# Attention masks of the second batch: from identity products on TensorE to additions on VectorE

## The chip, the cores and the metric

One core of a Trainium2 chip runs the whole program. The metric is the device time of one execution in microseconds (us); lower is better. PE is TensorE's matmul stream and PEld its weight loads, DVE is VectorE, ACT ScalarE, POOL GpSimd and SP the engine that issues most transfers.

## What is computed

Two batches of causal attention with 8 heads, 576 positions and 64 values per head, then two feed-forward layers over the 1152 tokens. Heads 0 to 3 see the last 32 positions ("local"), heads 4 to 7 the positions that agree with theirs modulo 32 ("strided").

```python
scores = scale * np.matmul(q, k.transpose(0, 1, 3, 2))
mask_local = (rel >= 0) & (rel < stride)
mask_strided = (rel >= 0) & (pos[None, :] % stride == pos[:, None] % stride)
scores = np.where(masks[None, :, :, :], scores, -1000000000.0)
scores = scores - np.max(scores, axis=-1, keepdims=True)
attn = np.exp(scores)
attn = attn / (np.sum(attn, axis=-1, keepdims=True) + 1e-09)
return np.matmul(attn, v).astype(np.float32)
# then x = attention output as [tokens, 512]:
#   four experts: sum over e of p[:, e] * (relu(x @ w1[e]) @ w2[e])
#   a gated layer: (sigmoid(x @ w_gate) * (x @ w_val)) @ w_out
```

## The kernel before

**Groups and stages.** Attention is cut into 32 groups, 16 for each batch. A strided group holds four blocks of 72 x 72 scores (288 values on each of 72 partitions), a local group three blocks of 96 x 128 (384 values on each of 96 partitions). The groups pass through the stages of `STAGES`, one group a step: scores (for two groups at every second step, `pair_scores`), maximum and exponentials (`group_exp`), normalisation one step later (`group_norm`), transposition three steps later (`group_transpose`), products with the values at five (`group_values`), and the split into a high and a low half, `xh` and `xl` (`group_split`). The generator `attention` gives this order, and `attend` takes one step of it.

**Scores.** `pair_scores` takes a bank of PSUM for each of the two groups. In each it first multiplies the identity by the mask (line 723, `start=True`), which writes 0 or -1e9 into every score, and then adds the products of queries and keys block by block (line 736, `start=False`). Three banks named `sps` serve all groups. `group_exp` lets VectorE take the negated row maximum from the bank (`nm`); ScalarE then exponentiates block by block, with `nm` as bias and the row sum into `sm`. `group_norm` adds 1e-9 to the sums and inverts them on VectorE (two short instructions on `sm`), and GpSimd multiplies (`P` by `sm`).

**What runs between.** The first batch's attention runs almost alone. The second batch's steps are mixed into the first four matrix stages (`early_up` and `early_down`, first expert, first 384 tokens): after each step of a stage (three products, lines 893 to 895) a share of 0.36 of an attention step is due. These stages need weights in two halves: ScalarE copies the raw weight (`wh`), GpSimd subtracts (`wl`, used by line 895). One piece of that work follows every second step of a stage. The results of `early_up` are evacuated by ScalarE (`hh`) and then VectorE (`hl`), those of `early_down` by VectorE into `x2acc`. Four PSUM banks (`gp`) serve these stages, the transposes of queries and keys (`qkps`), of probabilities (`tps`), and a few others.

**Order.** The order on each engine is that in which the program issues, and each engine keeps its order. `Ledger` books an estimated cost for every instruction of VectorE, ScalarE and GpSimd. After the attention, the order of background work follows from this account; the account's clock is then set to the latest of the three engines (line 1349) and all later decisions are made against that clock. During the attention, the order is that of `attend` and of `early_step`. Instructions of these three engines pass through a helper, so their rows all carry its line, 102, and are told apart by their tiles.

Of the kernel before, what the change touches and what calls it, by code (L numbers as in the profile page):

```python
# [17 lines left out]
ALU = mybir.AluOpType  # L18
# [89 lines left out]
def attn_moe_glu_kernel(ctx, tc, q, k, v, dp, w1, w2, wg, wv, wo, out):  # L108
    nc = tc.nc
    ledger = Ledger()  # L110
    dve, act, pool_ = (Reckoned(e_, name, ledger) for e_, name in ((nc.vector, "V"), (nc.scalar, "A"), (nc.gpsimd, "G")))
# [136 lines left out]
    identb = const.tile([128, 128], BF16, tag="identb", name="identb")  # L248
# [447 lines left out]
    def qk_local(b, part):  # L696
        for nm, dst in (("ql", QT), ("kl", KT)):
# [13 lines left out]
            else:  # L711
                dve.tensor_copy(dd, ps[:, :384])

    def pair_scores(pair):


        tiles = []
        for kind, b, c, half, hh in pair:
            ps = sp_.tile([128, 512], F32, tag="s", name="sps")
            n, w, m = (NU, NU, 4) if kind == "s" else (96, 128, 3)  # L720
            pv_ = ps[:n, :m * w].rearrange("p (a b) -> p a b", b=w)
            mask = mask_s.unsqueeze(1).to_broadcast([NU, 4, NU]) if kind == "s" else mask_l[:, half:half + 3, :]
            nc.tensor.matmul(pv_, identb[:n, :n], mask, start=True, stop=False)  # L723
            soft[kind, b, c, half, hh] = (pv_, n, w, m)
            tiles.append(pv_)
        m = soft[pair[0]][3]
        for j in range(m):
            for pv_, (kind, b, c, half, hh) in zip(tiles, pair):
                if kind == "s":
                    lo = 64 * half  # L730
                    qs_, ks_ = QT["s", b, c, hh][lo:lo + 64, j, :], KT["s", b, c, hh][lo:lo + 64, j, :]
                else:
                    lo, i = 64 * c, 3 * half + j
                    q0, k0 = hh * S + 96 * i, hh * S + max(96 * i - 32, 0)
                    qs_, ks_ = QT["l", b][lo:lo + 64, q0:q0 + 96], KT["l", b][lo:lo + 64, k0:k0 + 128]
                nc.tensor.matmul(pv_[:, j, :], qs_, ks_, start=False, stop=j == m - 1)  # L736

    def group_exp(g):
        pv_, n, w, m = soft[g]
        nm = atp.tile([128, 4], F32, tag="nm", name="nm", bufs=4)  # L740
        sm = atp.tile([128, 4], F32, tag="sm", name="sm", bufs=4)
        pt = atp.tile([128, 384], F32, tag="P", name="P", bufs=3)
        pp = pt[:n, :m * w].rearrange("p (a b) -> p a b", b=w)
        dve.tensor_reduce(nm[:n, :m], pv_, AX.X, ALU.max, negate=True)
        for j in range(m):
            act.activation(
                pp[:, j, :], pv_[:, j, :], AF.Exp, bias=nm[:n, j:j + 1], accum_out=sm[:n, j:j + 1]
            )
        soft[g] = (pp, sm[:n, :m], n, w, m)
# [72 lines left out]
    def attention():  # L822

        gs = []
        for b in range(B):
            gs += [("s", b, c, half, hh) for c in range(2) for hh in range(2) for half in range(2)]
            gs += [("l", b, c, half, hh) for half in range(2) for hh in range(2) for c in range(2)]
        n = len(gs)
        stage = dict(values=group_values, transpose=group_transpose, scores=pair_scores,
                     exp=group_exp, norm=group_norm, split=group_split)  # L830

        def ends():
# [583 lines left out]
```

## Time and profile before

| | |
|---|---|
| median of 3 runs | 649.19 us (648.48 to 649.87) |
| the profiled execution's own time | 648.63 us |
| its span, first to last instruction | 646.9 us |
| busy: PE / DVE / ACT / POOL | 636.3 / 438.7 / 341.9 / 266.7 us |
| granted TensorE clock | 0.999 of full speed |

The profile records one execution; its own time is 1.7 us longer than its span. Times in it are counted from the first instruction. A busy time is a union of intervals; what an engine waited for is inferred from semaphores. Second-batch scores are computed between 45.8 and 87 us; before that lie the first batch's attention and the loads, behind it the matrix stages to the end.

### The profile page before, as it was taken

To read this page: it belongs to the slowest core of one execution; us is meant where nothing else is said; L and a number is where in the kernel's file an instruction comes from. 1 tells how busy PE (TensorE), PEld (TensorE's weight loads), DVE (VectorE), ACT (ScalarE), POOL (GpSimd) and SP (SyncE) were. 2 spreads that over 40 slices of the span, in tenths; PEclk is the share of its full clock that TensorE was granted. 3 is DMA by queue.
4 is the path that set the end of the run, shared out by engine and by line. 5 is a ranking of instruction groups with operands and counts; after the bars stand their busy time and mean duration, and the time that the engine had idled before them with its cause. 6 is when DMAs were issued, how large, how long until landed. Compare 5 with 4: busy or idle time off the path is not lost.

```text
span 646.9 us, 12698 instructions
## 1 busy us (share of the span) xinstructions
PE 636.3 (98%) x4897; PEld 468.1 (72%) x4897; DVE 438.7 (68%) x882; ACT 341.9 (53%) x808; POOL 266.7 (41%) x311
## 2 busy tenths in 40 slices
PE   8889999999999999999999999999999999999998
PEld 5678889999676666666666666667978877987794
DVE  4876677787461886693887779898866759633432
ACT  6757643554753646775655454653565574542230
POOL 4675661000422325361435345440465367453540
PEclk9999999999999999999999999999999999999999
DMA  9976131040431544261674564254113832330002
GB/s 185 231 167 158 41 121 35 1 130 2 143 109 34 175 132 159 97 191 34 197 261 131 171 213 147 99 163 146 35 34 122 292 141 76 106 131 1 33 19 98
DMA packets 48884, 77.00 MB, mean 119 GB/s; under 512 B 19540, under 2 KB 24440, under 8 KB 47672
## 3 DMA queue, kind: packets, MB, share of 16 engines
q1 hardware_dynamic: 48824, 76.20, 38.7%
q8 instruction: 38, 0.62, 0.4%
q14 instruction: 22, 0.18, 0.1%
HBM read 59.66 MB, written 16.53 MB: 118 GB/s over the span
## 4 chain that ended last, share of the span: by engine, by line
PE 95%; DVE 3%; ACT 1%; issue 1%; POOL 0%; POOLq 0%; ACTq 0%
PE gps L893 23%; PE gps L895 23%; PE gps L894 23%; PE gps L997 19%; PE sps L736 1%; PE o L786 1%; PE tps L762 1%; ACT P L102 1%; PE warm L265 1%; DVE nm L102 1%; DVE sm L102 1%; PE qkps L682 0%; PE sps L723 0%; PE qkps L704 0%; DVE xh L102 0%
## 5 line engine op out<-in xcount | busy, mean ns | idle before, releaser
L102 POOL TENSOR_TENSOR hl<-t,hh 128x384 f16<-128x384 f32 x72 | 76.6, 1067 | 178.1 <-ACT t L102 174.2
L997 PEld LDWEIGHTS <-w 128*128 128x128 f16 x1512 | 125.0, 98 | 1.8
L997 PE MATMUL gps<-x,w 128*128 128x192 f16 x1512 | 126.2, 246 | 0.0
L893 PE MATMUL gps<-x,w 128*128 128x384 f16 x288 | 93.9, 326 | 0.0
L894 PE MATMUL gps<-x,w 128*128 128x384 f16 x288 | 93.9, 326 | 0.0
L895 PE MATMUL gps<-x,w 128*128 128x384 f16 x288 | 93.9, 326 | 0.0
L893 PE MATMUL gps<-hh,w 128*128 128x384 f16 x288 | 93.9, 326 | 0.0
L894 PE MATMUL gps<-hl,w 128*128 128x384 f16 x288 | 93.9, 326 | 0.0
L895 PE MATMUL gps<-hh,w 128*128 128x384 f16 x288 | 93.9, 326 | 0.0
L893 PEld LDWEIGHTS <-w 128*128 128x128 f16 x576 | 56.4, 98 | 37.3 <-issue 0.2
L895 PEld LDWEIGHTS <-w 128*128 128x128 f16 x576 | 56.4, 98 | 37.2
L894 PEld LDWEIGHTS <-w 128*128 128x128 f16 x576 | 56.4, 98 | 36.4
L102 ACT ACTIVATE hh<-gps 128x384 f16<-128x384 f32 (+1 forms) x96 | 46.7, 486 | 49.2 <-PE gps L895 48.8
L102 POOL TENSOR_TENSOR stage<-magn,stage 128x512 f16<-128x512 f32 x36 | 45.4, 1268 | 45.3 <-ACT magn L102 38.9
L102 ACT ACTIVATE w<-raw,up 128x512 f16<-128x512 f32 x48 | 32.0, 715 | 34.9 <-DVE up L102 34.8
L102 ACT ACTIVATE P<-sps,nm 72x72 f32<-72x72 f32 (+1 forms) x112 | 36.3, 331 | 23.7 <-DVE sm L102 15.6
L102 ACT ACTIVATE bits<-raw 128x512 f32<-128x512 f32 x36 | 24.3, 674 | 38.1 <-DVE magn L102 37.8
L102 DVE SCALAR_TENSOR_TENSOR w<-raw,up,w 128x512 f16<-128x512 f32 x48 | 40.1, 871 | 5.1 <-ACT w L102 4.9
L102 POOL TENSOR_TENSOR sg<-four,sg 128x384 f32<-128x384 f32 x9 | 9.8, 1093 | 80.6 <-DVE four L102 80.6
L893 PE MATMUL gps<-w,hh 128*128 128x512 f16 (+1 forms) x112 | 41.6, 371 | 0.0
L895 PE MATMUL gps<-w,hl 128*128 128x512 f16 (+1 forms) x112 | 41.6, 371 | 0.0
L894 PE MATMUL gps<-w,hh 128*128 128x512 f16 (+1 forms) x112 | 41.6, 371 | 0.0
(146 smaller groups left out, 1278.9 us busy)
## 6 DMA issues: line engine op xcount, KB each, us to landing
raw<-in_moe_w_dram SPq DMA_DIRECT2D x32, 512.0 KB
raw<-in_moe_w_gate_dram SPq DMA_DIRECT2D x12, 512.0 KB
raw<-in_moe_w_val_dram SPq DMA_DIRECT2D x12, 512.0 KB
raw<-in_moe_w_out_dram SPq DMA_DIRECT2D x12, 512.0 KB
wg<-stage SPq DMA_DIRECT2D x21, 256.0 KB
wv<-stage SPq DMA_DIRECT2D x21, 256.0 KB
w<-wg SPq DMA_DIRECT2D x3, 1024.0 KB
wo<-stage SPq DMA_DIRECT2D x12, 256.0 KB
```

The costliest lines, as they stand in the source:

```text
L102: return f(*a, **k)
L265: nc.tensor.matmul(ps, zero.to_broadcast([128, 128]), zero.to_broadcast([128, 512]), start=True, stop=True,)
L736: nc.tensor.matmul(pv_[:, j, :], qs_, ks_, start=False, stop=j == m - 1)
L762: nc.tensor.transpose(pv_[:, j, :], pp[:, j, :], ident[:n, :n])
L786: nc.tensor.matmul(o[x * 64:x * 64 + 64, j * n:(j + 1) * n], lhsT, tts[x][:, j, :], start=True, stop=True)
L893: nc.tensor.matmul(ps, ah, bh, start=first and i == 0, stop=False)
L894: nc.tensor.matmul(ps, ah, bl, start=False, stop=False)
L895: nc.tensor.matmul(ps, al, bh, start=False, stop=last and i == n - 1)
L997: nc.tensor.matmul(o, l_, r_, start=first and x + kk + y == 0, stop=last and x * kk * y == 2, skip_group_check=True)
```

## The change

In groups of the second batch (`b > 0`) the product of identity and mask is no longer issued. Every score block is then written by a product of its own with `start=True`. Ahead of the maximum, `group_exp` adds the mask to the scores on VectorE, which reads the bank and writes the same bank. The mask stays in its SBUF tile of type bfloat16 (for the strided groups repeated by its access pattern). The first batch keeps the products.

```diff
+    masks = {}
+
     def pair_scores(pair):
...
-            nc.tensor.matmul(pv_, identb[:n, :n], mask, start=True, stop=False)
+            if b == 0:
+                nc.tensor.matmul(pv_, identb[:n, :n], mask, start=True, stop=False)
+            else:
+                masks[kind, b, c, half, hh] = mask
             soft[kind, b, c, half, hh] = (pv_, n, w, m)
...
-                nc.tensor.matmul(pv_[:, j, :], qs_, ks_, start=False, stop=j == m - 1)
+                nc.tensor.matmul(pv_[:, j, :], qs_, ks_, start=b > 0, stop=b > 0 or j == m - 1)
...
     def group_exp(g):
...
+        if g in masks:
+            dve.tensor_tensor(pv_, pv_, masks.pop(g), ALU.add)
         dve.tensor_reduce(nm[:n, :m], pv_, AX.X, ALU.max, negate=True)
```

## Rows read from the trace of the kernel before

**Rows 1.** The page: the chain that ended last, by engine.
```profile
PE 95%; DVE 3%; ACT 1%; issue 1%; POOL 0%; POOLq 0%; ACTq 0%
```
**Rows 2.** Stretches: window, length, busy us of PE, PEld, DVE, ACT, POOL; clock, DMA.
```profile
44.00:55.00 11.00, 10.04 (x96) 8.89 (x95) 5.96 (x15) 7.30 (x32) 4.97 (x5) 1.00 0.83 189
55.00:65.00 10.00, 10.00 (x104) 8.97 (x102) 7.01 (x20) 6.91 (x36) 5.89 (x7) 1.00 0.34 104
75.00:91.00 16.00, 16.00 (x149) 13.51 (x148) 10.44 (x30) 9.54 (x40) 11.58 (x14) 1.00 0.17 47
```
**Rows 3.** Chain in order of time, mask products: start us, us on the chain, what.
```profile
45.99 0.25 PE sps L723 x2
...
68.05 0.33 PE sps L723 x2
```
**Rows 4.** DVE in order of time: start us, us, instruction, [idle before <-releaser].
```profile
39.24 0.46 DVE L102 TENSOR_TENSOR xl<-o,xh 128x288 fp32r<-128x288 f32 x1
...
50.56 0.16 DVE L102 TENSOR_SCALAR sm<-sm 72x4 f32<-72x4 f32 x1
50.75 0.17 DVE L102 RECIPROCAL sm<-sm 72x4 f32<-72x4 f32 x1
51.20 0.45 DVE L102 TENSOR_REDUCE nm<-sps 72x4 f32<-72x288 f32 x1 [0.28 <-PE sps L736]
...
94.00 0.52 DVE L102 TENSOR_TENSOR t<-gps,p 128x384 f32<-128x384 f32 x1
```
**Rows 5.** DVE by line and shape, 44 to 100 us: busy, mean ns | idle before.
```profile
L102 DVE TENSOR_TENSOR x2acc<-x2acc,t 128x384 f32<-128x384 f32 x4 | 3.3, 836 | 0.1
```
**Rows 6.** Chain in order of time, 46.9 to 55 us.
```profile
46.96 0.45 DVE nm L102
...
51.84 1.40 ACT P L102 x9
...
54.56 0.47 PE qkps L682 x4
```
**Rows 7.** Chain in order of time: the two waits for a low weight half.
```profile
70.10 0.18 PE gps L894
70.28 0.28 PE gps L895
...
88.77 0.41 PE gps L895
```
**Rows 8.** POOL in order of time: the subtractions that those waits end with.
```profile
68.78 1.28 POOL L102 TENSOR_TENSOR wl<-raw,wh 128x512 fp32r<-128x512 f32 x1 [0.19 <-ACT wh L102]
...
87.41 1.27 POOL L102 TENSOR_TENSOR wl<-raw,wh 128x512 fp32r<-128x512 f32 x1
```
**Rows 9.** DVE in order of time, 65 to 85 us: turns with ScalarE and TensorE.
```profile
65.58 0.45 DVE L102 COPY PT<-tps 72x288 f32<-72x288 f32 x1 [0.99 <-PE tps L762]
...
72.15 0.45 DVE L102 COPY PT<-tps 72x288 f32<-72x288 f32 x1 [1.41 <-PE tps L762]
...
75.57 0.44 DVE L102 COPY PT<-tps 72x288 f32<-72x288 f32 x1
76.09 0.55 DVE L102 TENSOR_REDUCE nm<-sps 96x3 f32<-96x384 f32 x1
...
78.29 0.56 DVE L102 SCALAR_TENSOR_TENSOR hl<-gps,hh 128x384 fp32r<-128x384 f32 x1 [1.37 <-ACT hh L102]
78.92 0.46 DVE L102 COPY PT<-tps 128x288 f32<-128x288 f32 x1
...
81.39 0.55 DVE L102 TENSOR_REDUCE nm<-sps 96x3 f32<-96x384 f32 x1 [0.42 <-PE sps L736]
...
83.59 0.56 DVE L102 SCALAR_TENSOR_TENSOR hl<-gps,hh 128x384 fp32r<-128x384 f32 x1 [1.17 <-ACT hh L102]
84.21 0.46 DVE L102 COPY PT<-tps 128x288 f32<-128x288 f32 x1
84.58 0.54 DVE L102 TENSOR_REDUCE nm<-sps 96x3 f32<-96x384 f32 x1
```

## Prediction

> **What bounds the kernel now.** I read the page's chain first: 95% of the span, followed back from its end, is TensorE's work [rows 1], so each microsecond that TensorE loses or saves counts in full unless another engine gives it back. Then the stretches in which the second batch's scores are made: TensorE has no idle time in two of them and about 1 us in the first (10.04 busy of 11) [rows 2]. VectorE is busy for 54 to 70% there, so by its share it has room. Shares hide the order, so I went on to the chain and to VectorE in order of time. There the work goes in turns: VectorE takes a maximum, ScalarE exponentiates, then evacuates `hh`, and only then can VectorE take `hl` and go on to its next copy and maximum. VectorE's longest gaps end with ScalarE's `hh` (1.37 and 1.17 us) [rows 9]. ScalarE was late there because its exponentials had waited for a maximum, so an addition in front of that maximum makes these gaps move, and does not fill them. Three more views matter: between 47 and 54.6 us the chain runs through VectorE and ScalarE, not TensorE [rows 6]; and twice TensorE waits for a low weight half that GpSimd is just finishing: its line 895 takes 0.28 and 0.41 us on the chain, where the product before the first of them takes 0.18 [rows 7], and GpSimd's subtractions end at 70.06 and 88.68 [rows 8], right before.
>
> **The change, part by part.**
>
> *Removed from TensorE.* 16 mask products in 8 pairs. A strided pair takes 0.25 us of the chain, a local pair 0.33 [rows 3]: 4 x 0.25 + 4 x 0.33 = 2.3 us. The `start` flags of the score products move no work, and no transfer is added or moved.
>
> *Added to VectorE.* 16 additions, 8 of 288 values and 8 of 384. The trace has none that writes PSUM. The nearest rows are sums of a PSUM bank and an SBUF tile written to SBUF: 0.46 us at 288 values, 0.52 at 384; a longer form of 384 values takes 0.56 [rows 4, 9]. I take 0.46 and 0.55. The maximum reads what the addition wrote; such a pair shows in the sums, where the reciprocal starts 0.03 us after the end of the instruction it reads [rows 4]. So one addition delays its maximum by 0.49 or 0.58 us, and all 16 by 8.6 us. Below, I bound the price by the 0.45 us of the maximum, which reads the same bank [rows 4], with the wait 0.48; above, by the sums `x2acc`, 0.84 us at 384 values [rows 5], hence 0.63 at 288, and with the wait 0.87 and 0.66. I stay near the PSUM sums, whose operands are most alike. That writing the bank costs as much as writing SBUF is my assumption; the bounds cover it.
>
> *What lies on the path.* I follow how late each step comes compared with before.
>
> 1. 46 to 54.6 us. The first pair's scores end 0.25 us earlier; the first addition makes the first maximum 0.24 late. Exponentials, a weight copy, `hh` and `hl` follow without a gap, so the second maximum, with its own addition, is 0.73 late. The third maximum ended at 51.65 [rows 4]; with the queue 0.73 late and its own 0.49 it ends at 52.87. The run of nine exponentials that began at 51.84 [rows 6] then comes about 1.0 late, and with it `hh`, `hl`, and TensorE at 54.56. The second pair's 0.25 us on TensorE is lost in this wait.
> 2. 55 to 65 us. TensorE is the bound (10.00 of 10.00). Two strided pairs give back 0.5 us. VectorE, 7.01 busy of 10 [rows 2], takes 4 additions, 1.96 us, and stays below full, but its evacuations in front of the next transposes come over 1 us late; I allow 0.1 for them. TensorE is 0.6 late at 65.
> 3. 65 to 70 us. VectorE's copy at 65.58 waited 0.99 us for TensorE [rows 9], so it is as late as TensorE: 0.6. The next addition, 0.49, makes it 1.1. From there maximum, exponentials, a copy of keys or queries, the weight copy and GpSimd's subtraction at 68.78 (it started as soon as ScalarE allowed) lead to TensorE at 70.1 [rows 7, 8]: 1.1 late. The local pair's 0.33 saved at 68 is swallowed by this wait.
> 4. 70 to 88.7 us. VectorE's copy at 72.15 again waited for TensorE (1.41 us) [rows 9]: 1.1 late. From there to the normalisation in front of GpSimd's last subtraction (87.41 [rows 8]) VectorE and ScalarE take turns, and five maxima lie on this path, at 72.5, 76.1, 79.3, 81.4 and 84.6: 5 x 0.58 = 2.90. Slack on it [rows 9]: the maximum at 76.09 started 0.52 after the copy before it where 0.37 is enough (84.21 to 84.58), 0.15; the one at 81.39 waited 0.42; the copies at 78.92 and 84.21 started 0.07 and 0.06 after `hl` ended, where an unhindered start is 0.09 before the end (84.21 + 0.46 against 84.58), 0.31 together. So 2.90 - 0.88 = 2.0, and line 895 at 88.74 comes 3.1 late. Here again what TensorE saves on three local pairs becomes waiting.
>
> Behind 88.7 no second-batch weight half is outstanding in these early stages and TensorE's work is as before, so the 3.1 us stay to the end. Seven of the 16 additions cost nothing: they fall into VectorE's waits for TensorE, such as the 0.99 and 1.41 us above; if that cover went, they would add up to 3.9 us. The account of `Ledger` books the additions too, but its decisions after the attention are made against a clock set to its latest engine, so I take the later order as unchanged.
>
> *Sum.* +1.0 - 0.5 + 0.1 + 0.49 + 2.0 = 3.1 us. The profiled execution (span 646.9, 1.7 us around it, 648.63) would become 651.7; it lies 0.56 under the median of 649.19, so I forecast 649.19 + 3.1 = 652.3.
>
> **Rivals.** 0.2% of the time, 1.3 us, is about what a measurement can tell from no change.
>
> *Hidden additions, faster.* VectorE has 5.0, 3.0 and 5.6 us idle in the three stretches of [rows 2], together more than the 8.6 us that it must take. If the turns stretch into it and the two weight waits do not grow, TensorE keeps its 2.3 us: 646.9. This decides if fewer than about four of the nine additions above delay the path. Against it: the gaps end with ScalarE [rows 9], which waits for the maximum. Chance 0.07.
>
> *The weight halves come in time.* GpSimd is busy 11.58 of 16 us [rows 2]; if its subtractions are not reached late, points 3 and 4 vanish but for one transpose that waits for a bank behind a late copy (0.58): 1.0 - 0.5 + 0.1 - 4 x 0.33 + 0.58 = -0.1, so 649.1. Against it: in [rows 7] both are late already. Chance 0.15.
>
> *Longer additions.* With 0.66 and 0.87, the upper bound, point 1 gives 1.5 (the third maximum ends at 51.65 + 1.07 + 0.66 = 53.38 against 51.84), point 2 leaves 1.1, point 3 makes 1.8, point 4 adds 5 x 0.87 - 0.88 = 3.5: 5.3, so 654.5. Chance 0.10. The Trainium skill, "VectorE: DVE Perf Modes", section "The DRAIN you can't avoid", comes near this price: after each instruction the pipeline empties for about its duration less 266 ns before the next one starts, by which 0.46 and 0.55 become 0.65 and 0.83 (an estimate with that page). The trace does not bear this out: the reciprocal starts 0.03 us after its predecessor's end, and the maximum at 84.58 before the copy's end [rows 4, 9].
>
> **How the numbers follow.** My forecast has 0.68. Slower by over 0.2%: forecast and longer additions less a little that falls short of 650.5, 0.75. Within 0.2%: the weight halves in time and that little, 0.17. Faster: 0.08. The range 649.5 to 655.0 reaches up past the longer additions and down into the second rival, and leaves out the hidden additions and about half of that rival.
>
> **What would show it.** Right: additions of 0.46 and 0.55 us on VectorE, each maximum 0.03 behind; TensorE idle near 53 us longer by about a microsecond; line 895 near 91.8 us waiting some 2 us for GpSimd; the distance from there to the end unchanged. Wrong: no wait at that weight half (second rival), additions of 0.6 us or more (third), or a later stretch whose order on the engines has changed.

## The result and the profile after

The changed kernel takes 655.39 us (median of 5 runs, 655.27 to 655.48). The kernel before took 649.87 us in the runs counted with it (648.48 to 652.63). The ratio is 1.0076, 95% interval 1.0051 to 1.0101: slower by 3.3 to 6.6 us, where 3.1 were forecast. The profiled execution has a span of 653.7 us against 646.9.

The page of the changed kernel, its chain by engine, answers to [rows 1]; TensorE has lost 3 points to VectorE, ScalarE and GpSimd.

```profile
PE 92%; DVE 4%; ACT 2%; POOL 1%; issue 1%; POOLq 0%; ACTq 0%
```

VectorE's groups by shape, 44 to 106 us: the 16 additions, busy time, mean ns of one | idle before.

```profile
L102 DVE TENSOR_TENSOR sps<-sps,ml 96x384 f32<-96x384 f32 x8 | 4.4, 552 | 0.4 <-PE sps L741 0.4
L102 DVE TENSOR_TENSOR sps<-sps,ms 72x288 f32<-72x288 f32 x8 | 3.6, 452 | 0.9 <-PE sps L741 0.9
```

They cost 0.45 and 0.55 us, as sums that read PSUM and write SBUF did (0.46 and 0.52 in [rows 4], 0.56 in [rows 9]). Writing the bank adds nothing that shows.

To place the loss I compare two events that every kernel here has: VectorE's first `hl`, which lies ahead of the first changed instruction, and the end of GpSimd's last subtraction of a weight half, for which line 895 (902 in the changed kernel) waits. Rows in order of time of the changed kernel, VectorE and GpSimd:

```profile
47.52 0.56 DVE L102 SCALAR_TENSOR_TENSOR hl<-gps,hh 128x384 fp32r<-128x384 f32 x1 [0.94 <-ACT hh L102]
...
94.12 1.26 POOL L102 TENSOR_TENSOR wl<-raw,wh 128x512 fp32r<-128x512 f32 x1
```

Before, the first `hl` starts at 43.90 and the last subtraction ends at 87.41 + 1.27 = 88.68 [rows 8]. After, it is 47.52 and 95.38. So of the 6.8 us between the two spans 3.6 stand ahead of the changed work and 3.1 in it (47.86 us from event to event against 44.78); the rest, 558.2 and 558.3 us to the end, did not move.

The 3.6 us ahead are no work of the change: up to here the order of the instructions is the same in both programs. Of the 3.6 us, 0.8 are there already at VectorE's second copy into `ksT` (8.44 against 7.59 us), while the clock is at 1.00. The other 2.8 come with a lower clock. Stretches of the changed kernel and, behind it, of the kernel before (window, length, busy us of PE, PEld, DVE, ACT, POOL; granted clock; DMA share, GB/s):

```profile
36.00:44.00 8.00, 7.21 (x51) 6.15 (x52) 4.65 (x14) 5.02 (x18) 6.86 (x8) 0.57 0.58 143
```
```profile
36.00:44.00 8.00, 7.84 (x81) 7.09 (x82) 6.21 (x21) 4.45 (x14) 6.86 (x8) 1.00 0.81 192
```

TensorE ran most of this stretch at 1.2 GHz in the one execution and at 2.4 GHz in the other.

Behind the first `hl`, TensorE in order of time, the rows that end a wait:

```profile
58.10 0.42 PE L769 MATMUL tps<-ident,P 72*72 72x72 f32 x4 [2.05 <-DVE ksT L102]
...
74.71 0.45 PE L902 MATMUL gps<-xh,wl 128*128 128x384 f32 x1 [0.41 <-POOL wl L102]
...
93.51 0.44 PE L900 MATMUL gps<-hh,wh 128*128 128x384 f32 x1 [0.44 <-ACT hh L102]
94.10 0.44 PE L901 MATMUL gps<-hl,wh 128*128 128x384 f32 x1 [0.15 <-DVE hl L102]
95.44 0.44 PE L902 MATMUL gps<-hh,wl 128*128 128x384 f32 x1 [0.89 <-POOL wl L102]
```

The first of these waits stood before too, at 53.7, with 0.80 us. Between the two events TensorE is busy for 42.76 us where it was busy for 43.67, and idle for 5.1 us where it was idle for 1.1. What it no longer multiplies, it waits, and 3.1 us more.

VectorE in order of time at one turn (lines of the forecast's point 4):

```profile
83.96 0.56 DVE L102 SCALAR_TENSOR_TENSOR hl<-gps,hh 128x384 fp32r<-128x384 f32 x1 [1.39 <-ACT hh L102]
84.43 0.45 DVE L102 COPY PT<-tps 128x288 f32<-128x288 f32 x1
84.80 0.55 DVE L102 TENSOR_TENSOR sps<-sps,ml 96x384 f32<-96x384 f32 x1
85.38 0.55 DVE L102 TENSOR_REDUCE nm<-sps 96x3 f32<-96x384 f32 x1
```

They answer to the rows from 78.29 us on in [rows 9]. The wait for `hh` is as long as before (1.39 against 1.37), the copy now starts 0.09 us before the end of `hl` where it started 0.07 behind it, and the maximum starts 0.03 us after the addition's end (84.80 + 0.55 to 85.38). The idle time of VectorE has moved and has not been filled.

### The profile page after: what moved, and what is told of

Its sections match the earlier page's. It is cut to its first block, busy times and chain, and to the rows that moved or that the text cites. A ratio compares the mean times of both kernels' runs of the same rounds, so it can differ in the third digit from the quotient of the medians.

```text
span 653.7 us, 12686 instructions
## 1 busy us (share of the span) xinstructions
PE 639.2 (98%) x4881; PEld 469.5 (72%) x4881; DVE 445.8 (68%) x898; ACT 341.9 (52%) x808; POOL 267.0 (41%) x311
## 4 chain that ended last, share of the span: by engine, by line
PE 92%; DVE 4%; ACT 2%; POOL 1%; issue 1%; POOLq 0%; ACTq 0%
PE gps L900 22%; PE gps L902 22%; PE gps L901 22%; PE gps L1004 19%; ACT P L102 2%; PE o L793 1%; PE tps L769 1%; PE warm L265 1%; PE sps L741 1%; DVE nm L102 1%; DVE PT L102 1%; DVE sm L102 1%; PE qkps L682 1%; DVE sps L102 0%; DVE hl L102 0%
```

## The experiments

All numbers "event to event" run from the start of the first `hl` to the end of the last subtraction of a weight half, read from the one profiled execution of each run:

| run | first `hl` | last subtraction ends | event to event | less before |
|---|---|---|---|---|
| kernel before | 43.90 | 88.68 | 44.78 | |
| kernel before, again | 44.16 | 88.91 | 44.75 | 0.0 |
| before, waits filled | 44.98 | 89.79 | 44.81 | 0.0 |
| no masks | 44.12 | 87.61 | 43.49 | -1.3 |
| strided groups on VectorE | 47.47 | 93.23 | 45.76 | +1.0 |
| local groups on VectorE | 47.77 | 94.63 | 46.86 | +2.1 |
| changed kernel | 47.52 | 95.38 | 47.86 | +3.1 |
| changed, waits filled | 44.98 | 92.82 | 47.84 | +3.1 |
| changed, again (clock fell at 56 us) | 44.92 | 94.18 | 49.26 | +4.5 |
| products and additions, waits filled | 44.80 | 93.33 | 48.53 | +3.8 |
| products and additions (clock fell at 58 us) | 45.80 | 95.86 | 50.06 | +5.3 |
| every addition twice, waits filled | 44.85 | 98.80 | 53.95 | +9.2 |

**The kernel before, and the changed kernel, again.** No edit.

> The kernel before, once more, with a profile. In the profiles at hand the changed kernel is 6.8 us longer, and 3.6 of these stand ahead of the first changed instruction: VectorE's first hl starts at 43.90 before and at 47.52 after, and TensorE's granted clock is 0.50 to 0.67 between 36 and 44 us. Theory A: those 3.6 us belong to the chip and the moment, not to the change; this run can show them too (first hl at 47 to 48 us and a low clock near 38 us, about 652.5 in all), and from the first hl to the end it takes 603.0 us as before. Theory B: the change brings them by its layout of code; this run shows the first hl near 43.9 and about 649.2.

> The changed kernel, once more. Theory A (turns of VectorE and ScalarE, 3.1 us): 3.1 us, 0.48%, longer than the kernel before on the same chip, 606.2 us from the first hl to the end. Theory B (the whole difference comes from the change): 5.5 us, 0.85%, longer.

The kernel before took 651.45 us in 12 executions and 650.48 in 23 more, from 648.45 to 652.63, with a mean granted clock of 1.000 to 0.992. The profiled one had a clock of 1.00, its first `hl` at 44.16 and 648.87 us, as theory B expected. But the slower of the other executions have the lower clock (0.995 or less in all above 651.9), and with two waits of the first batch filled both the low clocks and the long times are gone (run before_fill, below). So a fall of the clock in the first batch does not need the change. Whether the change makes it more frequent stays open: with unfilled waits, all five profiles of kernels with additions show one between 32 and 44 us, and none of the three without.

The changed kernel took 655.38 us, ratio 1.0078 (1.0052 to 1.0105), 4.9 us over the median beside it. This lies between the two theories, near B. Its profile shows one reason why the 3.1 us are not all. Stretches of the changed kernel, run again:

```profile
52.00:56.00 4.00, 1.95 (x20) 1.65 (x18) 3.15 (x9) 3.47 (x19) 2.55 (x3) 1.00 0.64 177
56.00:60.00 4.00, 3.82 (x20) 3.61 (x18) 2.63 (x8) 1.81 (x10) 1.90 (x2) 0.57 0.40 129
```

TensorE stands idle for half of the first window, the same wait of 2.05 us, and at a clock of 0.57 in the second. From event to event this execution needs 49.26 us, 1.4 more than the first profile, in which the same wait, ending at 58.10, was followed by a clock of 1.00:

```profile
56.00:60.00 4.00, 1.76 (x17) 1.59 (x17) 3.16 (x8) 2.82 (x15) 2.05 (x3) 1.00 0.30 75
60.00:64.00 4.00, 4.00 (x41) 3.63 (x40) 2.80 (x10) 2.52 (x16) 2.47 (x3) 1.00 0.15 58
```

**Parts of the change alone.** First, no masks at all in the second batch (edit of the changed kernel):

```diff
             else:
-                masks[kind, b, c, half, hh] = mask
+                pass
```

> The second batch's masks are left out altogether: no product and no addition. Theory A: TensorE saves at most 2.3 us, and part of that is lost where it waits for ScalarE, VectorE or the weight halves; 1.4 to 2.3 us shorter than before. Rival (the product fills time in which TensorE waits anyway): no shorter than before.

Then products and additions both (edit of the kernel before):

```diff
+    masks = {}
...
             nc.tensor.matmul(pv_, identb[:n, :n], mask, start=True, stop=False)
+            if b:
+                masks[kind, b, c, half, hh] = mask
...
+        if g in masks:
+            dve.tensor_tensor(pv_, pv_, masks.pop(g), ALU.add)
         dve.tensor_reduce(nm[:n, :m], pv_, AX.X, ALU.max, negate=True)
```

> The products stay and the additions are made as well, so the second batch's masks count twice. Theory A: the additions alone cost the walk without TensorE's saving, 3.1 plus about 0.8, so 4.0 us longer than before, 0.6%. Rival (additions hidden): no longer than before. Rival (all 16 additions on the path): 8.6 us longer.

Without masks the ratio is 0.9982 (0.9964 to 1.0), and from event to event 1.3 us go, a little less than the 1.4 to 2.3 expected and not the 2.3 us that the products take on the chain. TensorE's idle time between the events grows from 1.1 to 1.9 us, so most of the rest becomes waiting.

With both, the ratio is 1.0063 (1.004 to 1.0087), about 4.1 us as expected; from event to event the profiled execution needs 5.3 us more, and there the clock had fallen at 58 us, behind a wait of 1.79 us. The median of 654.22 us is no higher than that of the changed kernel, which does less work (655.38; the intervals overlap). Falls of the clock blur differences of this size, hence the same kernel with the waits filled (the edit is shown further down):

> Products and additions both (masks count twice), with the waits filled as in the run after_fill, so that the clock stays up. Theory A: the additions alone cost the walk without TensorE's saving, about 4.0 us: 48.7 us from the first hl to the last weight half against 44.8 before, and no fall of the clock between 45 and 96 us; some 653.5 in all. Rival (hidden additions): 44.8 us. Rival (all 16 on the path): 53.4 us.

It needs 48.53 us, 3.8 more than before (ratio 1.0058, 1.0035 to 1.0081), and no clock fell between the events (it fell behind them, at 94 us). So additions cost 3.8, and taking the products away then gives back only 0.7 of the 2.3 us (3.8 to 3.1).

**Strided or local groups alone** (the condition for products becomes `not (b and kind == "s")`, or `"l"`, and the flags of the score products follow it).

> Only the strided groups of the second batch get their masks from VectorE; the local groups keep the products. Theory A (turns): points 1 and 2 of the walk remain and end 0.6 us late at 65 us, and later waits add a little: from the first hl to the last weight half 45.4 to 45.9 us against 44.8 before. Rival (every addition costs the same share of the 3.1): 46.3 us. A fall of the clock near 56 us adds 1.4.

> Only the local groups get their masks from VectorE. Theory A: points 3 and 4 without the strided addition at 66 us: five additions of 0.58 less 0.9 of slack, 2.0 to 2.3 us: from the first hl to the last weight half 46.8 to 47.1 us, no wait of 2 us at 54 us and no fall of the clock there. Rival (equal shares): 46.3 us.

1.0 and 2.1 us (45.76 and 46.86 from event to event), both within what was expected, and together the 3.1 us of the whole change. The rival of equal shares falls: eight additions of 0.49 cost half of what eight of 0.58 cost. The cost follows the place, not the number. Each of these two kernels was executed once (653.4 and 656.5 us, with a fall of the clock in the first batch in both), so their whole times decide nothing.

**Filling the waits.** Dummy products in two waits of the first batch, for both kernels; for the changed one also ten products of zeros, accumulated into the bank in use, ahead of the wait of 2.05 us (`cur[0]` holds that bank).

```diff
-EMPTY = {..., **{i: 2 for i in range(5, 16, 2)}, 16: 1}
+EMPTY = {..., **{i: 2 for i in range(5, 16, 2)}, 13: 6, 15: 8, 16: 1}
...
             at_step[0] = i
+            if i == 24:
+                for _ in range(10):
+                    nc.tensor.matmul(
+                        cur[0], zero.to_broadcast([128, 128]), zero.to_broadcast([128, TC]), start=False, stop=False)
```

> The kernel before with ten more of its dummy products of zeros in two waits of TensorE in the first batch (1.30 us at 29.6 and 1.76 us at 34.2), 4 x 0.22 and 6 x 0.22 us, so within the waits. Theory A: the falls of TensorE's granted clock between 32 and 44 us follow these waits and come and go between executions; with the waits filled the clock stays at 1.00, all runs lie at 648.5 to 649.3, the median some 1.5 us under that of before. Rival (the falls have nothing to do with the waits): the same spread of 648.5 to 652.6 as before. From the first hl to the end of the last subtraction of a weight half 44.8 us either way.

> The changed kernel with the same ten dummy products, and ten products of zeros (0.16 us each) added to the bank that is being accumulated, right ahead of the wait of 2.05 us that stands near 54 to 56 us in the changed kernel. Theory A: no fall of the clock at 56 to 62 us, from the first hl to the last weight half 47.8 to 48.0 us, and 3.1 us longer than the kernel before with its waits filled: 651.8 to 652.4. Rival (the falls have nothing to do with the waits): 655.4 as the changed kernel, falls as before. Rival (the zeros delay TensorE): over 48.5 us in that stretch.

The kernel before with filled waits had a mean clock of 0.999 or 1.000 in all 12 runs; the 23 runs beside it had 1.000 to 0.992. Its times drew together (648.77 to 650.18 against 648.22 to 652.59), but the median did not fall, 649.62 against 649.22, ratio 0.9987 (0.9969 to 1.0005): the expected 1.5 us were missed. Its profile has the first `hl` 1.1 us later than before, which is no work of the filled waits, since TensorE had waited for a transfer ahead of them:

```profile
17.86 0.72 PE L786 MATMUL o<-PT,vs 72*64 72x72 f32 x16 [1.02 <-DMA vs<-in_v_dram]
```

The changed kernel with filled waits, TensorE in order of time and the stretches:

```profile
53.35 1.82 PE L868 MATMUL gps<-const-float32-0.0 128*128 128x384 bf16 x10
55.57 0.42 PE L769 MATMUL tps<-ident,P 72*72 72x72 f32 x4 [0.39 <-DVE ksT L102]
```
```profile
52.00:56.00 4.00, 3.61 (x30) 2.55 (x29) 3.09 (x10) 3.40 (x19) 2.55 (x3) 1.00 0.03 10
56.00:60.00 4.00, 3.81 (x40) 3.35 (x39) 3.55 (x11) 1.90 (x10) 1.90 (x2) 1.00 0.36 129
```

The zeros take 1.82 us of the wait and delay nothing: event to event 47.84 as without them, and the clock stays at 1.00. The median is 652.9, 2.5 us under that of the changed kernel (measured on another chip), and 3.3 over that of the kernel before with filled waits (on the same chip). Half of its runs still have a mean clock of 0.997, where a fall may have been left. What it cost is not known: the kernel before has 0.997 in some of its fastest runs too. In the runs with local groups and with both masks, waits filled, the profile shows a fall at 94 to 98 us, behind the waits for `hh` and the weight half, which were not filled; the longest of them is 0.93 us.

**Every addition twice**, waits filled (twenty products of zeros).

```diff
+            dve.tensor_tensor(pv_, pv_, masks[g], ALU.add)
             dve.tensor_tensor(pv_, pv_, masks.pop(g), ALU.add)
```

> The changed kernel with every addition made twice (the second batch's masks count twice), waits filled, twenty products of zeros in the long one. Theory A: where VectorE and ScalarE take turns each further 0.49 or 0.58 us counts nearly in full on the path, since the slack of 0.9 us is used up by the first: 9 further additions, 4.9 us and up to 2 us more where additions that were hidden come to the surface: 52.5 to 54.8 us from the first hl to the last weight half. Rival (additions mostly hidden, the cost being a fixed one of the changed order): 47.8 to 49 us.

53.95 us, as expected: the second 16 additions cost 6.1 us, the first 3.8 (with the products kept) or 3.1. Of 8.6 us that they take on VectorE, 71% now stand on the path. The rival, a fixed cost of the changed order, falls. In this execution, the only one (661.6 us), the clock fell at 95 us, within the measured stretch. Even so the 6.1 us hold: the last turn, in which it fell, grew by 1.04 us against the kernel before (from `hl` to `hl`), and the 0.45 of the changed kernel and 0.58 for the second addition account for that. What the fall cost came behind, where the rest to the end is 2.8 us longer.

**Weight halves sooner**, in both kernels with filled waits.

```diff
-                        if n_step[0] % 2:
+                        if n_step[0] % 3:
                             early_step(n)
```

> The changed kernel with waits filled as in after_fill, and two pieces of weight preparation in three steps in place of one in two, so that the low weight halves are done earlier. Theory A: the waits of TensorE for the weight halves at 72 and 92 us (1.3 us together) go, and from the first hl to the end it takes 605.0 to 605.5 us against 606.1; the turns of VectorE and ScalarE still leave 2 us of the 3.1. Rival (the loss belongs to the weight halves alone): 603 us or less. Rival (ScalarE's earlier copies stand before exponentials and cost as much): 606 us or more.

> The kernel before with its waits filled as in before_fill and two pieces of weight preparation in three steps, as in prep_sooner. Theory A (sooner preparation pays because the additions had pushed the weight halves behind TensorE): here the waits for weight halves are only 0.1 to 0.3 us, so nothing is gained: span 647.7 to 648.3 against 648.0, median 649.3 to 649.9, and the changed kernel with the same edit (651.2) stays 1.4 to 1.9 us slower. Rival (sooner preparation is worth 1.5 us in any case): median 648.1, the fastest version of all.

This moves the last subtraction, so only the time from the first `hl` to the end can be compared. It is 603.9 us for the changed kernel (649.6 - 45.70), a miss: lower than the 605.0 to 605.5 expected. But the edit itself also moves the first `hl`: in the kernel before, that time becomes 602.2 (647.9 - 45.73) where it was 603.0, with the span unchanged (647.9 against 648.0). Against that the changed kernel is 1.8 us longer (before rounding), where without the edit it was 3.1. TensorE in order of time, its waits between 70 and 92 us in the changed kernel with this edit:

```profile
76.24 0.42 PE L769 MATMUL tps<-ident,P 72*72 72x72 f32 x4 [0.71 <-POOL P L102]
87.62 0.44 PE L769 MATMUL tps<-ident,P 96*128 96x96 f32 x3 [0.76 <-DVE hl L102]
90.57 0.44 PE L906 MATMUL gps<-hh,wh 128*128 128x384 f32 x1 [0.42 <-ACT hh L102]
91.16 0.44 PE L907 MATMUL gps<-hl,wh 128*128 128x384 f32 x1 [0.15 <-DVE hl L102]
```

Both waits for a weight half are gone (0.41 and 0.90 us with filled waits alone), and 1.3 of the 3.1 us are gone with them. Other waits changed too (the one for `hl` from 0.21 to 0.76 us), so that the two sums are equal is not yet a proof. All 10 runs had a clock of 1.000 and the median is 651.2, 1.7 under the changed kernel with filled waits. The kernel before gains nothing from it: 650.04, ratio 1.0004 (0.9991 to 1.0018). The two medians are 1.2 us apart, on different chips, where 1.4 to 1.9 were expected. No version with the masks in place beats the kernel before by more than the measurement can tell.

## Why the forecast was right in kind and short in size

The forecast held in direction and place. Its four points, measured in the first profile with the 3.62 us ahead taken off:

1. At the transpose at 54.56, forecast 1.0 late. It starts at 58.96 on the chain: 0.8. The third maximum had waited 0.28 us for TensorE ([rows 4] show it) and I had not counted that as slack.
2. At 65 us, forecast 0.6. The transposes at 65.1 stand at 69.26: +0.5.
3. At the first weight half, forecast 1.1: the product at 70.12 starts at 74.71, 1.0.
4. At the last weight half, forecast 3.1: its subtraction ends at 95.38 in place of 88.68, 3.1. From there to the end nothing changes (558.2 and 558.3 us).

The sum of the turns, 3.1 us, was thus measured as 3.1, and the runs with half of the change, with the products kept, and with twice the additions bear out its terms. That it agrees to a tenth is in part luck: the first three points came 0.1 to 0.2 us earlier than forecast, and the last stretch added 2.1 in place of 2.0. One sign was wrong in size: line 895 was to wait some 2 us for GpSimd near 91.8, and waited 0.89 us there (95.44 less 3.62), since TensorE had waited 0.44 and 0.15 us for `hh` and `hl` just before. And the additions that cost nothing come to 3.7 us by their own prices (4 x 0.49 + 3 x 0.58), not 3.9; nothing in the sum rests on that.

Rival one, hidden additions, fell: TensorE waits. Rival two, weight halves in time, fell in the changed kernel as it stands, and an edit that made it come true took 1.3 us back. Rival three fell by the rows: additions of 0.45 and 0.55, maxima 0.03 to 0.04 us behind them, which also speaks against an emptying of the pipeline in between. The reciprocal that I had held against it could not: by the rule quoted there, its predecessor of 0.16 us leaves nothing to empty.

What the sum lacked is a term for TensorE's clock. I read a clock of 1.00 in all stretches of [rows 2] and took a wait to cost its own length. The changed kernel has a wait of 2.05 us where there were 0.80; behind it the clock fell to 1.2 GHz in one of the two profiles, and that cost 1.4 us (49.26 against 47.86). In the other, the one of the first comparison, the loss beyond the 3.1 us stands ahead of the change: 0.8 by 8 us and 2.8 at the low clock. The measured difference, 5.1 us by the second ratio, is thus 3.1 of turns and about 2 more. That falls of the clock make up most of these 2 follows from the runs with filled waits, in both kernels, where the difference of the medians is 3.3; the profile shows one place, at 56 us. How much stands there and how much in the first batch, and whether the change makes the falls of the first batch more frequent, was not separated. Of the unprofiled runs the mean clock alone is known, 0.997 to 0.987 for the changed kernel on a chip where the kernel before had 1.000 to 0.992.

In the first comparison the runs of the kernel before were not all of one kind: three lay at 648.5 to 649.9 and two at 652.5 to 652.6. Beside the latter the changed kernel is 2.8 us slower. The forecast of 652.3 and its range, 649.5 to 655.0, started from the median of 649.19. By the ratio that median becomes 654.1 us, inside the range; the 655.39 themselves lie 0.4 above it.

## What to carry to other kernels

An engine's idle share is no room for new work when its idle time ends with another engine that waits for it in turn: walk the turn, count each addition in front of the step that both need, subtract the slack found in the rows, and expect the saved work on the bounding engine to come back as waiting. Where that engine is TensorE, ask which of its waits grow, because a clock that falls behind one is a cost beyond the wait, and one that comes and goes between executions. Products of zeros laid into such a wait cost nothing here (47.84 us against 47.86) and the clock stayed up behind them; they do not shorten the turn.

## What the hardware showed that I had not expected

In one execution of the changed kernel TensorE's granted clock was 1.00 from 36 us up to a wait of 2.05 us and 0.57 in the 4 us from 56 us on, right after it. In another execution with the same wait it stayed at 1.00 behind it. The level that it falls to is 1.2 GHz of 2.4 (0.50 between 37 and 42 us in the first profile). Nor does the length of one wait decide: with both masks and filled waits the clock was at 0.50 between 95 and 97 us, soon after a wait of 0.92 us, and in the kernel before a wait of 1.76 us at 34.2 was followed by 1.00. The Trainium skill, "TensorE: Matmul & The Clock Gate", section "What's actually happening", says of the rise of the clock that the same kernel, from run to run, has a different number of slow products at its start. No run here shows such a start; what differed here was whether a fall came at all. With 1.82 us of the wait filled with products of zeros the clock stayed at 1.00 in the profiled execution, and in the first batch ten dummy products brought the mean clock of the kernel before to 0.999 or 1.000 in all 12 runs.
